# Experts' operands at one distance of 64 bytes, later casts of the row sums, and two short 32-bit products

## The chip, the cores and the metric

The kernel runs on one core of one Trainium2 chip. The metric is the device time of one execution in microseconds (us), the median over several runs. The engines are named as the profile names them: PE is TensorE's matmul, PEld its weight load, DVE is VectorE, ACT is ScalarE, POOL is GpSimd, SP is SyncE, which issues most of the DMAs.

## What is computed

The input is 8 sequences of 2496 tokens of 256 numbers. A Fourier layer mixes each sequence: real transform, a complex 256x256 product with a bias, a soft threshold, inverse transform. Its result goes through a mixture of 8 experts, in which every token takes one expert.

```python
X = np.fft.rfft(x, axis=1)
Yr = Xr @ w_r - Xi @ w_i + b_r
Yi = Xr @ w_i + Xi @ w_r + b_i
Y = soft_threshold(Yr, 0.01) + 1j * soft_threshold(Yi, 0.01)
x = np.fft.irfft(Y, n=2496, axis=1).reshape(19968, 256)

e_idx = argmax(x @ w_gate + modality_bias[modality_id])
for e in range(8):                       # w1: 8 x 256 x 1024, w2: 8 x 1024 x 256
    h = maximum(x[e_idx == e] @ w1[e], 0)
    out[e_idx == e] = gate_w * (h @ w2[e])
```

## The kernel before

The first 597 us are the Fourier layer and the routing: each sequence is transformed by matmuls, and its rows are scattered by expert into a table `xs` in HBM. The rest of the span is class `Experts`, and the change lies there.

**Units.** The experts' rows are worked on in 40 units, counted from 0: 38 of 512 rows and 2 of 256. Every operand is split into a rounded high part and a remainder (`xh`, `xl`; `hh`, `hl`; two slots in each weight tile), so a product of two matrices is three matmuls in a 32-bit format that TensorE takes in one pass, each with 128x128 stationary and 256 moving columns. Layer one (line 1024) holds the weights `w` stationary and streams `xh` or `xl`; layer two (line 1095) holds `hh` or `hl` stationary and streams `w`. From unit 8 on (`NPL` = 8) layer one is done with sums of rows and columns in 7 products in place of 8. A unit below 8 has 96 matmuls of layer one and 96 of layer two; units 8 to 37 have 84 and 96; the last two have 48 and 48. That makes 768 + 2520 + 96 = 3384 of layer one and 3648 + 96 = 3744 of layer two, 7128 in all.

**The order.** It is written out by hand in `run`. A unit has two groups (`grp` 0 and 1). In each, products of layer one of one half and of layer two of another take turns by the string that `order` gives ("1212..."; each "1" or "2" is 6 matmuls). After step n of a group the tables `FILL`, `FILL1`, `FILL2` say which side work is issued: "x" is one part of the next unit's split (an ACT cast to `xh`, line 958, and a POOL subtraction to `xl`, line 959), "t" the sums of rows on DVE, "o" an output, "p" DVE transposes for the unit after. Engines take their work in this order. Every sixth unit from unit 14 on also carries a small tile of at most 32 rows (`tiny`), whose few 32-bit matmuls stand between those blocks of 6.

**Where the operands lie.** Two sets of weight tiles take turns by the parity of the unit: set 1 lies behind the tiles of `xh`/`xl` and `hh`/`hl` on the left side of SBUF, set 0 at its right end. `PADS` shifts pools by a few floats. All tiles are multiples of 512 bytes long or are read at offsets that are, so an operand's start, taken modulo 512 bytes within its partition, is the same for all its slices. In the program as built these are:

| operand | role | before | after, odd unit | after, even unit |
|---|---|---|---|---|
| `xh`, `xl` | moving in layer one | 416 | 384 | 384 |
| `w0`, `w1` | stationary in layer one | 480 | 448 | 480 |
| `w2`, `w3` | moving in layer two | 480 | 384 | 416 |
| `hh`, `hl` | stationary in layer two | 416 | 448 | 448 |

While one matmul streams its moving operand, PEld loads the stationary operand of the next.

**Pads.** `setup_pads` fills a tile with a marker row; `pads` writes it behind each expert's rows, with the generator `late` as the caller, stepped once after some steps of a group (`LATE`).

Of the kernel before, what the change touches and what calls it, by code (L numbers as in the profile page):

```python
# [9 lines left out]
F32 = mybir.dt.float32  # L10
F32R = mybir.dt.float32r
# [12 lines left out]
D = 256  # L24
# [7 lines left out]
GC = D + E  # L32
# [8 lines left out]
TINY = 32  # L41
SLOTS = 5
MORE = 16
NPL = 8
EARLY = (6 * SEQ - 8 * (TP - 1)) // TP + 1 - E
PADS = (56, 16)
W1 = 2 * 2 * 4 * 128
W2 = 2 * 4 * 256
RAW = (2, 4, 6, 8, 10)
# [747 lines left out]
class Experts:  # L797
# [8 lines left out]

    def sets(self, ctx, i, **k):
        p = ctx.enter_context(self.tc.tile_pool(name=f"mw{i}", bufs=1, reuse_waits="tile", **k))
        return [p.tile([128, 2, 2, 7, 128] if n < 2 else [128, 2, 4, D], F32R, name=f"w{n}_{i}") for n in range(4)]

    def pools(self, ctx):
        nc, tc, rt = self.nc, self.tc, self.rt
        pool = lambda name, bufs, **k: ctx.enter_context(
            tc.tile_pool(name=name, bufs=bufs, reuse_waits="tile", **k))
        pad = lambda name, n: n and pool(name, 1).tile([128, n], F32, name=name + "t")
        self.x = pool("mx", 2)
        self.tr = pool("mtr", 1)
        self.cp = pool("mc", 1)
        self.ident = self.cp.tile([128, 128], F32, name="mident")
        nc.gpsimd.memset(self.ident, 0.0)  # L820
        nc.gpsimd.affine_select(out=self.ident, in_=self.ident, compare_op=ALU.not_equal, fill=1.0, base=0,
                                pattern=[[-1, 128]], channel_multiplier=1)
        pad("mq0", PADS[0])
        self.xp = pool("mxs", 1)
        self.s = pool("ms", 1)
        self.h = [pool("mh0", 1), pool("mh1", 1)]
        pad("mq1", PADS[1])
        self.wb.append(self.sets(ctx, 1))
        self.b = pool("mb", 2)
        room = rt.at.x1f[0]  # L830
        self.raw = (room[:, :2 * F].rearrange("p (c f) -> p c f", c=2),
                    room[:, 2 * F:2 * F + 8 * D].rearrange("p (c d) -> p c d", d=D))
        self.small, o = {}, 2 * F + 8 * D
        for nm, n in (("xt", GC), ("xc", 256), ("x", 256), ("hs", 256), ("h", 256), ("y", 256), ("ix", 1)):
            self.small[nm], o = room[:, o:o + n], o + n
        self.ps = pool("mps", 2, space=PSUM)
        self.hps = pool("mhps", 1, space=PSUM)
# [282 lines left out]
    def fill(self, n):  # L1120
# [3 lines left out]
        for _ in range(n):  # L1124
            self.nc.tensor.matmul(ps, tri[:, :128], tri[:, :512], start=True, stop=True)

    def put(self, ix, o):
        ins = self.nc.gpsimd.indirect_dma_start(  # L1128
            out=self.out, out_offset=bass.IndirectOffsetOnAxis(ap=ix, axis=0),
            in_=o, in_offset=None, bounds_check=NTOK - 1, oob_is_err=False)  # L1130
        self.tc.declare_no_dep(ins.ins, group="outs", reason="every token has one writer")
        self.tc.add_to_no_dep_group("outs", ins.ins)
# [74 lines left out]
    def sort_half(self, i):  # L1207
# [9 lines left out]
    FILL1 = {0: "x", 1: "o", 4: "x", 7: "x", 13: "x"}  # L1217
    FILL2 = {0: "x", 1: "o", 3: "t", 4: "x", 6: "x", 9: "x", 10: "x", 14: "x", 15: "x"}
    FILL = (
        {0: "x", 1: "o", 3: "t", 4: "x", 6: "xx", 8: "x", 11: "x", 13: "x"},  # L1220
        {1: "o", 3: "p", 5: "p"})
    LATE = (2, 3, 5, 7, 9, 10, 12)

# [9 lines left out]
    def run(self, late, *tail):  # L1233

        nc = self.nc
        U = NP + NS
        self.tags = {NPL - 1: [2, 4, 5, 6]}
        for i in range(NPL - 2, -1, -1):
            t = self.tags[i + 1]
            self.tags[i] = [t[3]] + [j for j in range(7) if j not in t]  # L1240
        pieces = self.weight_sums()
        for i in range(2):
            self.load_x(i)
        self.rt.setup_pads(self.cp.tile([128, GC], F32, name="pad2"))
        self.rt.grid2 = self.rt.load_grid(self.cp, "c_grid2", 5 * E + 3)
        for n in range(4):
            self.load_w(1, n)
            if n == 0:
                next(pieces)
        self.fold = self.cp.tile([128, TINY], F32, name="fold")  # L1250
        with self.tc.issue_after(tail[0].ins), self.tc.issue_after(tail[1].ins):
            for _ in chain(self.prep(0), self.sums(0), self.parts(0)):
                pass
        nc.vector.reduce_sum(self.fold, self.ident.rearrange("p (g t) -> p t g", t=TINY), AX.X)
        self.fill(5)
        for _ in self.layer1(0, 0):
            pass
        for _ in self.prep(1):
            pass
        every = (U - 8) // SLOTS  # L1260
        for i in range(U):
            if i + 2 < U:
                assert i + 2 < EARLY or self.rt.late
                if i == NPL - 2:
                    assert next(pieces, None) is None
                self.load_x(i + 2)
                self.load_w(i + 2, 0)
            k, at = divmod(U - 2 - i, every)
            k = U + SLOTS - 1 - k
            small = U <= k < U + SLOTS  # L1270
            if small and at == 2:
                self.load_x(k)
                self.stage = self.load_raw(k)
            if small and at == 1:
                self.sort_half(k)
            if small and at == 0:
                self.side = self.tiny(k)
            for grp in range(2):
                one = self.layer1(i + grp, 1 - grp) if i + grp < U else iter(())
                n1 = (8 if i + grp < NPL else 7 if i + grp < NP else 4) if i + grp < U else 0  # L1280
                n2 = 2 * self.subs(i)
                two = self.layer2(i, grp)
                fill = {"o": iter(()), "x": self.parts(i + 1) if grp == 0 and i + 1 < U else iter(()),
                        "t": self.sums(i + 1) if grp == 0 and i + 1 < U else iter(()),
                        "p": self.prep(i + 2) if grp == 1 and i + 2 < U else iter(())}
                if self.rest:
                    fill["o"], self.rest = self.last(*self.rest), None
                fills = self.FILL[grp] if grp or i >= NPL else self.FILL2 if i == NPL - 1 else self.FILL1
                for n, c in enumerate(self.order(n1, n2)):
                    next(one if c == "1" else two)  # L1290
                    for f in fills.get(n, ""):
                        next(fill[f], None)
                    if n in self.LATE:
                        next(late, None)
                    if i < NPL - 2:
                        next(pieces, None)
                    if c == "2":
                        next(self.stage, None)
                        if n % 3 == 0:
                            next(self.side, None)  # L1300
                for g in (one, two, fill["o"], fill["t"], fill["x"], fill["p"]):
                    for _ in g:
                        pass
                if i + 2 < U:
                    if grp == 0:
                        self.load_w(i + 2, 1)
                    self.load_w(i + 2, 2 + grp)
        for _ in self.side:
            pass
        self.finish(*self.rest)  # L1310

        k = U + SLOTS
        more = nc.values_load(self.rt.ti[k:k + 1, 3:4], min_val=0, max_val=1,
                              skip_runtime_bounds_check_because="a flag")
        with self.tc.If(more > 0):
            for i in range(k, k + MORE):
                self.load_x(i)
                for _ in self.load_raw(i):
                    pass
                self.sort_half(i)  # L1320
                self.half(i)
# [37 lines left out]
def build(tc, I, out, nb):  # L1359
    nc = tc.nc  # L1360
    with ExitStack() as outer:
# [218 lines left out]
        with ExitStack() as ctx:  # L1580
            ctx.enter_context(tc.manual_schedule(engines={ET.PE, ET.Activation, ET.DVE, ET.Pool}))
            ex.pools(ctx)

            def late():
                for state in chain(routing, rt.tiles_last(ex.cp)):
                    yield
                    if state == "pe":
                        for _ in range(3):
                            yield
                while rt.pending:  # L1590
                    rt.scatter(1)
                    yield
                    yield
                for _ in range(12):
                    yield
                rt.pads()
                for _ in range(8):
                    yield
                rt.fence()
                rt.late = True  # L1600


            ex.run(late(), *tail)
# [24 lines left out]
```

## Time and profile before

| | us |
|---|---|
| median of 3 runs | 1458.16 |
| lowest, highest | 1457.96, 1460.24 |
| the profiled execution | 1462.81 |
| its span, first to last instruction | 1460.9 |
| PE busy | 1427.8 |
| PEld busy | 1366.1 |
| DVE busy | 900.3 |
| ACT busy | 782.0 |
| POOL busy | 793.0 |

The profile is of one execution. Busy time of PE is the union of its matmuls, each of which is shown some 280 ns long though one starts about every 116 ns; what a matmul costs is therefore read from the distance between two starts. The timeline merges equal neighbours ("x2"), gives each row's start and length in us, and in square brackets the idle time ahead of it with what ended it.

### The profile page before, as it was taken

What the parts mean: (1) busy time and instruction counts of PE and PEld (TensorE: products, weight loads), DVE (VectorE), ACT (ScalarE), POOL (GpSimd) and SP (SyncE); (2) the same over time, 40 slices, a digit from 0 to 9 for tenths busy, and PEclk for the clock granted to TensorE, in tenths of its full rate; (3) what the DMA queues carried; (4) which work ended last, traced back from release to release, by engine and by line L of the source; (5) the groups of instructions that cost most, each with busy time, mean ns of one, the idle gap of its engine ahead of it and who ended that gap; (6) DMA issues with size and microseconds to landing.
All of it is one profiled execution on the core that took longest, in us unless ns stands there. A gap on an engine that the chain in (4) does not pass through costs nothing. (4 is left out here: it accounts for less than half of the span.)

```text
span 1460.9 us, 33883 instructions
## 1 busy us (share of the span) xinstructions
PE 1427.8 (98%) x12084; PEld 1366.1 (94%) x12084; DVE 900.3 (62%) x1721; ACT 782.0 (54%) x1675; POOL 793.0 (54%) x907
## 2 busy tenths in 40 slices
PE   8899999999999999999999999999999999999996
PEld 5889999998989999999999999999999999999995
DVE  4567575757575876667565665666566656665651
ACT  3465656565656454544445555555555555555542
POOL 2355767676767666366667543444344444444432
PEclk9999999999999999999999999999999999999998
DMA  8979686969696759687787288124122942682192
GB/s 265 264 236 297 212 284 214 298 215 299 200 297 182 224 180 290 198 248 249 240 277 245 70 291 268 38 59 115 32 60 58 338 126 59 203 261 59 44 355 80
DMA packets 245299, 289.82 MB, mean 198 GB/s; under 512 B 121232, under 2 KB 176267, under 8 KB 241925
## 3 DMA queue, kind: packets, MB, share of 16 engines
q1 hardware_dynamic: 225587, 244.64, 54.4%
q0 software_dynamic: 19408, 42.83, 9.3%
q8 instruction: 98, 1.61, 0.5%
q14 instruction: 76, 0.62, 0.1%
q10 hardware_dynamic: 130, 0.12, 0.0%
HBM read 322.80 MB, written 117.56 MB: 301 GB/s over the span
## 5 line engine op out<-in xcount | busy, mean ns | idle before, releaser
L1095 PE MATMUL y<-w,hh 128*128 128x256 f32 x2496 | 461.4, 279 | 0.0
L1095 PEld LDWEIGHTS y<-w,hh 128*128 128x128 f32 x2496 | 380.8, 189 | 3.7 <-issue 3.7
L1095 PE MATMUL y<-w,hl 128*128 128x256 f32 x1248 | 346.8, 278 | 1.1 <-DVE hl L1030 0.9
L1024 PE MATMUL X<-xh,w 128*128 128x256 f32 x1248 | 270.3, 281 | 0.0
L1128 POOL DMA_INDIRECT out<-o,ix x156 | 155.4, 996 | 182.4 <-ACT o L1112 145.7
L1095 PEld LDWEIGHTS y<-w,hl 128*128 128x128 f32 x1248 | 234.2, 188 | 1.7 <-DVE hl L1030 1.7
L1024 PEld LDWEIGHTS X<-xh,w 128*128 128x128 f32 x1248 | 212.6, 188 | 2.0 <-ACT hh L1029 1.6
L1024 PE MATMUL X<-xl,w 128*128 128x256 f32 x624 | 174.6, 280 | 0.6 <-POOL xl L959 0.6
L1030 DVE SCALAR_TENSOR_TENSOR hl<-Y,hh 128x512 fp32r<-128x512 f32 x140 | 96.8, 692 | 102.9 <-ACT hh L1029 102.8
L1029 ACT ACTIVATE hh<-Y 128x512 fp32r<-128x512 f32 x140 | 83.8, 599 | 119.0 <-DVE Y L1033 101.1
L959 POOL TENSOR_TENSOR xl<-tr,xh 128x256 fp32r<-128x256 f32 x94 | 70.4, 749 | 129.2 <-ACT xh L958 128.7
L1024 PE MATMUL Z<-xh,w 128*128 128x256 f32 x608 | 131.8, 281 | 0.7 <-DVE Y L1033 0.7
L382 PE MATMUL mx<-wmix,Xh 128*128 128x256 f32 x640 | 116.6, 305 | 7.5 <-DVE mx L372 7.2
L959 POOL TENSOR_TENSOR xl<-xt,xh 128x256 fp32r<-128x256 f32 x122 | 89.5, 746 | 58.5 <-ACT xh L958 57.2
L1024 PEld LDWEIGHTS X<-xl,w 128*128 128x128 f32 x624 | 117.1, 188 | 1.0 <-POOL xl L959 0.8
L1038 ACT COPY v<-X 128x512 f32<-128x512 f32 x180 | 105.6, 587 | 17.5 <-PE X L1024 10.3
L598 POOL DMA_INDIRECT xs<-x1b,si x88 | 90.0, 1023 | 41.5 <-DVE pl L430 19.6
L424 PE MATMUL pv<-pv,z 128*120 128x136 f32 x704 | 108.5, 279 | 1.0 <-ACT z L414 0.9
L598 POOL DMA_INDIRECT xs<-x,si x88 | 89.5, 1017 | 36.0 <-issue 16.7
L292 POOL TENSOR_TENSOR x1l<-x,x1h 117x512 fp32r<-117x512 f32 x59 | 75.6, 1284 | 60.8 <-ACT x1h L290 21.9
L382 PEld LDWEIGHTS mx<-wmix,Xh 128*128 128x128 f32 x640 | 92.4, 190 | 16.4 <-ACT x1h L290 3.6
L1024 PEld LDWEIGHTS Z<-xh,w 128*128 128x128 f32 x608 | 103.7, 188 | 0.9 <-DVE Y L1033 0.9
(261 smaller groups left out, 3435.8 us busy)
## 6 DMA issues: line engine op xcount, KB each, us to landing
w<-wsp SPq DMA_DIRECT2D x96, 1024.0 KB
w<-wss SPq DMA_DIRECT2D x64, 1024.0 KB
w<-wsp SPq DMA_DIRECT2D x64, 768.0 KB
a<-scr SPq DMA_DIRECT2D x160, 128.0 KB
x<-in_x SPq DMA_DIRECT2D x38, 512.0 KB
xt<-xs SPq DMA_DIRECT2D x152, 128.0 KB
scr<-ev SPq DMA_DIRECT2D x35, 480.0 KB
wsp<-wh SPq DMA_DIRECT2D x64, 256.0 KB
```

The lines of the kernel that those rows point to most:

```text
L292: (nc.gpsimd if pool else nc.vector).tensor_sub(xl, x, xh)
L382: nc.tensor.matmul(mx[:, i, :], t[:, c, 1 - i, :], self.w[:, i, c, lo, :], start=False, stop=n == 5, skip_group_check=True)
L424: nc.tensor.matmul(ps[:PK, c * 128:c * 128 + D // 2 + E], self.z[:, o:o + 3, :, :].rearrange("p n k r -> p (n k r)"), self.pv[:, c, :], st ...
L598: i = self.nc.gpsimd.indirect_dma_start(out=self.xs, out_offset=bass.IndirectOffsetOnAxis(ap=si[:, k:k + 1], axis=0), in_=rows, in_offset= ...
L959: (nc.gpsimd if i or j in (0, 1, 6) else nc.vector).tensor_sub(sq(xl), v, sq(xh))
L1024: nc.tensor.matmul(ps[:, u, :], w1[:, lo, u, blk, :], x, start=start and u == k == 0, stop=k == 2, skip_group_check=True)
L1029: nc.scalar.activation(hh[:, par::2, o], v, AF.Relu)
L1030: nc.vector.scalar_tensor_tensor(hl[:, par::2, o], v, 0.0, hh[:, par::2, o], ALU.max, ALU.subtract)
L1038: nc.scalar.copy(v, ps)
L1095: nc.tensor.matmul(ps, h[:, q, o], w2[:, lo, q, :], start=grp == s % 2 == q == k == 0, stop=grp == 1 and q == 3 and k == 2, skip_group_che ...
L1128: ins = self.nc.gpsimd.indirect_dma_start(out=self.out, out_offset=bass.IndirectOffsetOnAxis(ap=ix, axis=0), in_=o, in_offset=None, bounds ...
```

## The change

Five things are done. (1) In `sets`, the tiles `w2`, `w3` are laid out ahead of `w0`, `w1`, with a tile of 64 bytes between them; `pools` moves the pad of 64 bytes ahead of `hh`/`hl` and adds one of 448 bytes behind. With the 1056 bytes of the tile `pad2`, which goes, this gives the starts in the table above. (2) `FILL`, the table of units from 8 on, issues the casts after the second one step later or two. (3) `part` is new: one product in full 32-bit format, `fold` (128x32) stationary and `ident` (128x128) moving, into a PSUM tile that nobody reads. It stands after the first block of layer one in group 0 of units 1 and 9. (4) `setup_pads` of the experts' stage is called from `late`, one step ahead of `pads`, into a piece of an older tile. (5) The list of pads has a third entry.

```diff
-PADS = (56, 16)
+PADS = (56, 16, 112)
...
-        return [p.tile([128, 2, 2, 7, 128] if n < 2 else [128, 2, 4, D], F32R, name=f"w{n}_{i}") for n in range(4)]
+        w2 = [p.tile([128, 2, 4, D], F32R, name=f"w{n}_{i}") for n in (2, 3)]
+        p.tile([128, 16], F32, name=f"mq2_{i}")
+        return [p.tile([128, 2, 2, 7, 128], F32R, name=f"w{n}_{i}") for n in (0, 1)] + w2
...
         self.s = pool("ms", 1)
+        pad("mq1", PADS[1])
         self.h = [pool("mh0", 1), pool("mh1", 1)]
-        pad("mq1", PADS[1])
+        pad("mq3", PADS[2])
         self.wb.append(self.sets(ctx, 1))
...
+    def part(self):
+
+        ps = self.rt.ps.tile([128, 512], F32, tag="r", name="part")[:TINY, :128]
+        self.nc.tensor.matmul(ps, self.fold, self.ident, start=True, stop=True)
...
-        {0: "x", 1: "o", 3: "t", 4: "x", 6: "xx", 8: "x", 11: "x", 13: "x"},
+        {0: "x", 1: "o", 3: "t", 4: "x", 7: "x", 8: "x", 10: "x", 12: "x", 14: "x"},
...
-        self.rt.setup_pads(self.cp.tile([128, GC], F32, name="pad2"))
...
+                    if n == 1 and grp == 0 and i in (1, NPL + 1):
+                        self.part()
                     next(one if c == "1" else two)
...
-                for _ in range(12):
+                for _ in range(11):
                     yield
+                rt.setup_pads(ex.small["xt"])
+                yield
                 rt.pads()
```

PE at the start of group 0 of unit 1, before. `X_1` is a PSUM bank of layer one's second half, `y_0` the output bank of layer two; `w_1` are weights of set 1.

```order
L1024 MATMUL X_1_8734<-xh_1_8415,w_1_8245 128x256
L1024 MATMUL X_1_8734<-xl_1_8416,w_1_8245 128x256
L1024 MATMUL X_1_8734<-xh_1_8415,w_1_8245 128x256 x2
L1024 MATMUL X_1_8734<-xl_1_8416,w_1_8245 128x256
L1024 MATMUL X_1_8734<-xh_1_8415,w_1_8245 128x256
L1095 MATMUL y_0_8748<-w_1_8246,hh_1_8559 128x256 x2
L1095 MATMUL y_0_8748<-w_1_8246,hl_1_8560 128x256
```

The same place of PE now (lines 1024 and 1095 have become 1027 and 1098).

```order
L1027 MATMUL X_1_8737<-xh_1_8418,w_1_8253 128x256
L1027 MATMUL X_1_8737<-xl_1_8419,w_1_8253 128x256
L1027 MATMUL X_1_8737<-xh_1_8418,w_1_8253 128x256 x2
L1027 MATMUL X_1_8737<-xl_1_8419,w_1_8253 128x256
L1027 MATMUL X_1_8737<-xh_1_8418,w_1_8253 128x256
L1133 MATMUL part<-mident,fold 32x128
L1098 MATMUL y_0_8753<-w_1_8249,hh_1_8562 128x256 x2
L1098 MATMUL y_0_8753<-w_1_8249,hl_1_8563 128x256
```

One 32-bit product has come between the first block of layer one and the first of layer two; the same is so in unit 9, and nothing else of PE's order differs.

ACT in group 0 of unit 9, before: `xh_10` are casts for unit 10, `v_9` and `hh_9` are the copies and the relu that empty layer one's banks.

```order
L958 CAST xh_10_11499<-tr_11316 128x256
L958 CAST xh_10_11518<-xt_11097 128x256
L958 CAST xh_10_11522<-xt_11097 128x256
L1038 COPY v_9_1_11538<-X_1_11438 128x512
L1029 ACTIVATE hh_9_11436<-Y_1_11439 128x2x256
L958 CAST xh_10_11543<-xt_11097 128x256
L1029 ACTIVATE hh_9_11436<-X_1_11438 128x2x256
```

The same place of ACT now.

```order
L961 CAST xh_10_11506<-tr_11321 128x256
L961 CAST xh_10_11531<-xt_11102 128x256
L1041 COPY v_9_1_11541<-X_1_11443 128x512
L1032 ACTIVATE hh_9_11441<-Y_1_11444 128x2x256
L961 CAST xh_10_11546<-xt_11102 128x256
L961 CAST xh_10_11566<-xt_11102 128x256
L1032 ACTIVATE hh_9_11441<-X_1_11443 128x2x256
```

The copy of a bank and the relu behind it have moved ahead of one cast; this repeats in units 8 to 38.

## Rows read from the trace of the kernel before

**Rows 1.** The page's first part: busy us, share of the span, instructions.
```profile
PE 1427.8 (98%) x12084; PEld 1366.1 (94%) x12084; DVE 900.3 (62%) x1721; ACT 782.0 (54%) x1675; POOL 793.0 (54%) x907
```

**Rows 2.** Windows, PE: stretch, length, busy (x), PEclk, DMA share, GB/s.
```profile
932.00:1038.00 106.00, 106.00 (x913) 1.00 0.30 71
```

**Rows 3.** Timeline, PE, unit 0: start us, us, engine line operation.
```profile
599.15 0.28 PE L1024 MATMUL Y<-xh,w 128*128 128x256 f32 x1
...
601.87 0.28 PE L1024 MATMUL X<-xh,w 128*128 128x256 f32 x1
```

**Rows 4.** Timeline, PE, where blocks of the two layers take turns.
```profile
643.63 0.39 PE L1095 MATMUL y<-w,hh 128*128 128x256 f32 x2
...
644.32 0.28 PE L1024 MATMUL Z<-xh,w 128*128 128x256 f32 x1
...
645.03 0.40 PE L1095 MATMUL y<-w,hh 128*128 128x256 f32 x2
...
645.74 0.28 PE L1024 MATMUL Z<-xh,w 128*128 128x256 f32 x1
...
646.43 0.39 PE L1095 MATMUL y<-w,hh 128*128 128x256 f32 x2
```

**Rows 5.** Timeline, PE, in a double block of layer two, unit 17.
```profile
992.09 0.40 PE L1095 MATMUL y<-w,hh 128*128 128x256 f32 x2
...
993.15 0.28 PE L1024 MATMUL X<-xh,w 128*128 128x256 f32 x1
```

**Rows 6.** Timeline, PE, a small tile's 32-bit products and layer one behind.
```profile
923.60 1.07 PE L1196 MATMUL y<-x 128*32 128x256 f32 x16
...
924.95 0.39 PE L1024 MATMUL X<-xh,w 128*128 128x256 f32 x2
...
925.40 0.39 PE L1095 MATMUL y<-w,hh 128*128 128x256 f32 x2
```

**Rows 7.** Timeline, PE, its last 32-bit product and layer two behind.
```profile
928.76 0.28 PE L1095 MATMUL y<-w,hl 128*128 128x256 f32 x1
928.97 0.62 PE L1202 MATMUL ysum<-x,fold 128*32 128x256 f32 x2
...
929.86 0.28 PE L1095 MATMUL y<-w,hl 128*128 128x256 f32 x1
...
930.33 0.28 PE L1024 MATMUL X<-xh,w 128*128 128x256 f32 x1
```

**Rows 8.** Timeline, PE, the two waits and what follows the second.
```profile
727.73 0.38 PE L1095 MATMUL y<-w,hl 128*128 128x256 f32 x1 [0.94 <-DVE hl L1030]
...
906.84 0.39 PE L1024 MATMUL Z<-xh,w 128*128 128x256 f32 x1 [0.71 <-DVE Y L1033]
...
907.18 0.40 PE L1024 MATMUL Z<-xh,w 128*128 128x256 f32 x2
...
907.53 0.28 PE L1024 MATMUL Z<-xh,w 128*128 128x256 f32 x1
```

**Rows 9.** Timeline, DVE, ahead of the same two waits.
```profile
726.31 0.43 DVE L983 TENSOR_TENSOR bs<-br 128x256 f32<-128x256 f32 x1 [5.66 <-issue]
...
904.89 1.30 DVE L910 STREAM_TRANSPOSE tr<-xt 128x512 f32<-128x512 f32 x2 [3.58 <-DMA xt<-xs]
```

**Rows 10.** Timeline, PE, a short pause without a wait.
```profile
1003.59 0.30 PE L1024 MATMUL X<-xh,w 128*128 128x256 f32 x1
1003.73 0.28 PE L1024 MATMUL X<-xl,w 128*128 128x256 f32 x1
```

**Rows 11.** Timeline, ACT, the two casts and the copy behind them.
```profile
1002.20 0.77 ACT L958 CAST xh<-xt 128x256 fp32r<-128x256 f32 x2 [1.62 <-POOL xl L959]
1002.87 0.58 ACT L1038 COPY v<-X 128x512 f32<-128x512 f32 x1
```

**Rows 12.** Line 614, the pads' fill: duration ns least/median/most, first and last start.
```profile
L614 POOL MEMSET pad<- x2: 309/330/351, 539.6 to 582.7; 128x264 f32 x2
```

**Rows 13.** Page, part 5, POOL's subtraction: count | busy us, mean ns | idle before, releaser.
```profile
L959 POOL TENSOR_TENSOR xl<-tr,xh 128x256 fp32r<-128x256 f32 x94 | 70.4, 749 | 129.2 <-ACT xh L958 128.7
```

## The prediction, made before the changed kernel ran

> **What bounds the kernel now.** I read the page's busy times first, then windows over the experts' stage, then the timeline of PE alone, start by start. PE is busy 98% of the span, DVE, the next, 62% [rows 1], and in 932 to 1038 us PE is busy for all of 106.00 us at the full granted clock [rows 2]. So nothing on another engine can shorten this stage unless PE's own matmuls start closer together. How close they start is the question. The window counts 913 matmuls that touch it; one is shown 0.28 us long, so their starts fill 106.28 us: 116.4 ns from start to start.
>
> That is a mean of two paces. In unit 0, where layer one runs alone, 24 products go from 599.15 to 601.87 us: 2.72 us, 113.3 ns each [rows 3]. In a double block of layer two 9 products go from 992.09 to 993.15: 117.8 ns each [rows 5]. Shape, number format and clock are the same. Where blocks of six take turns, four in a row take 0.69, 0.71, 0.71 and 0.69 us: layer two fast, layer one slow, layer two slow, layer one fast [rows 4]. So the pace changes each time layer one follows layer two (644.32, 645.74), and is kept each time layer two follows layer one (645.03, 646.43). The reader is to see that nothing waits there: it is an offset that the stream of matmuls carries on until something shifts it.
>
> **Why the operands' places would matter.** By the table of starts, inside a block of layer one PE streams from 416 while PEld loads from 480, and inside layer two the reverse. At a boundary both read from the same start: 416 and 416 going from one to two, 480 and 480 going from two to one. Only there, and only at the second kind, does the pace change. This is a reading of rows, no proof. After the change every pair, inside and across, streams from the 64 bytes that begin at 384 and loads from those that begin at 448 (even units lie 32 bytes further in some of them). If the reading holds, blocks no longer change the pace, and whatever pace an outside event leaves stays.
>
> **Which pace is left.** Behind the small tile's 16 short 32-bit products layer one starts fast: 4 products from 924.95 to 925.40, 112.5 ns [rows 6]. Behind its last 32-bit product, with the same `fold` as the new `part`, layer two starts slow: 4 from 929.86 to 930.33, 117.5 ns [rows 7]. Layer one is the case with the stream in the lower place; after the change layer two is so too, so I expect it fast behind both, and behind `part`.
>
> **The sum, by stretch.** A fast product gains 116.4 - 113.3 = 3.1 ns, a slow one loses 117.8 - 116.4 = 1.4 ns.
> Until `part` in unit 1 (about 626 us) I can't tell the pace: 0.
> From there to PE's wait at 727.73 [rows 8]: some 101 us, 865 products fast: -2.7 us.
> From that wait to `part` in unit 9 (about 803 us): behind the other wait layer one runs 3 products in 0.35 us, 117 ns [rows 8], so I take slow: 650 x 1.4 = +0.9.
> From 803 to the wait at 906.84: 880 products fast: -2.7.
> From there through the small tile at 929 [rows 7]: mixed, 0.
> Units 14 to 37 behind it: 24 x 180 = 4320 products. Four further small tiles cover some 155 products each; on these 620 I count half, -1.0; on the other 3700 -11.5. The last two units: 0.
> Together -17.0 us. The most there could be is 7128 x 3.1 = 22.1.
>
> **What is added.** *The two products.* From 928.76 to 929.86 stand one product ahead of `ysum`, `ysum` itself and two behind: 1.10 us where three products take 0.35, so 0.75 us for 256 moving columns [rows 7]. `part` has 128. Between half and all of it I take 0.5 each, nearer to the half, as the columns are: +1.0 (0.75 to 1.5). It is on the path, since PE has no gap.
>
> *Pauses.* At 1003.59 a matmul starts 0.14 us after the one ahead without a wait being shown [rows 10]; there is one more of this kind in the later units. Before, a changed offset was undone or repeated a block later; after, a slow one would stay until the next small tile, at most five units, half of that on average: 450 x 4.5 ns = 2.0 us. I count half of one such case, +1.0 (0 to 4).
>
> *The two waits.* PE waits 0.94 and 0.71 us for DVE [rows 8], and DVE in its turn had waited for data: 5.66 us ahead of an addition that reads a loaded tile, 3.58 us for the DMA of an `xt` [rows 9]. If these data come no earlier, what PE gained ahead of them, 2.7 us each time, is given back there. The loads are mostly issued behind PE's own steps and so move with it; I take +1.0 for both (0 to 5.4).
>
> *Casts.* ACT's copy of layer one's bank starts at 1002.87, behind two casts that began at 1002.20 [rows 11]; with one cast moved behind it, it starts some 0.37 us earlier. PE was not waiting for it [rows 2], so the gain is 0. The last cast moves from step 13 to 14, and DVE's transposes, which overwrite its source, come after step 3 of the next group: four blocks of 0.70 us, 2.8 us, less a cast of 0.4 [rows 11] and POOL's 0.75 [rows 13], leave 1.6 us. That room is the cover. Were it gone, the transposes would hold up the `hl` queued behind them on DVE, for which layer two waits: up to the 0.7 us of the shift in a unit, 31 times, 22 us. I see no row that points to it.
>
> *Pads.* The fill of 0.33 us [rows 12] moves on POOL's queue from the start of the stage to the step ahead of the pads. Behind it on POOL stand outputs, and SP's pad writes wait for it; units that read them come later. POOL is busy 54% [rows 1]: 0 to 0.4, I take 0.
>
> **Sum.** -17.0 + 1.0 + 1.0 + 1.0 = -14.0 us. The profiled execution took 1462.81, so 1448.8 for it; the median of the runs is 4.65 lower, 0.3%, and 1458.16 - 14.0 gives 1444.
>
> **Rivals.** *Slow pace kept.* The same mechanism, with the other outcome: behind `part` and the small tiles the common pace is the slow one, as layer two's was [rows 7], and now nothing flips it back. All products at 117.8 ns cost 7128 x 1.4 = 10.0 us, and `part` 1.0: 1469. It decides where the share of fast products falls under 1.4 / 4.5 = 31%; before, it is about that much, since the mean is 116.4 between 113.3 and 117.8. For it speaks that I know the outcome behind a 32-bit product only for the old places; against it, layer one's fast start [rows 6] in the very arrangement that is now common to all. Chance 0.16, of which 0.03 ends below 1461.
>
> *Places don't matter.* The flips come from something else, the alternation stays as it is, and `part` costs its 1.0: 1459. Against it speaks that only one of the two boundaries flips [rows 4], and that a run of one layer never does [rows 3]. Chance 0.10.
> [...]
>
> *Gain given back.* Fast pace, but both waits take all that was won ahead of them, 5.4 in place of 1.0, and two pauses leave the slow pace: 1444 + 4.4 + 3.0 = 1451. It lies within the forecast's case.
>
> **How the numbers follow.** The forecast's case, mostly fast, has 0.74. Its best end is 22.1 less 0.75, 1437; I leave 0.04 below 1438. Its worst, with small tiles leaving the slow pace now and then, is 1455. Range 1438 to 1461: left out are 0.04 below and 0.13 above. About 0.2% (3 us) is what a measurement of this kernel can tell from no change. Faster 0.74, same 0.10, slower 0.16.
>
> **What would show it.** In the changed profile, blocks of six all 0.68 us long in units 1 to 6, 9 to 12 and from 15 on, with no step where layer one follows layer two, would show the places' part right; one even length of 0.71 would show the slow rival, and 0.69, 0.71, 0.71, 0.69 as before the third. The first block behind `part` shows whether it sets the pace, and the first behind PE's waits near 727 and 906 us whether a wait unsets it. What would make the forecast wrong at its root is a slow pace behind the small tiles, since two thirds of the gain lie between them.

## The result, and the profile after

| | before | after |
|---|---|---|
| median, us | 1459.93 | 1470.71 |
| lowest, highest, us | 1457.96, 1461.46 | 1469.2, 1473.06 |
| span of the profiled execution, us | 1460.9 | 1468.2 |
| PE busy, us | 1427.8 | 1437.5 |

The changed kernel is slower: 1.0077 times the time before, 95% interval 1.0061 to 1.0092, or 10.8 us, where 14 us less was forecast. The page's first part of after, to lay beside [rows 1]:

```profile
PE 1437.5 (98%) x12088; PEld 1375.7 (94%) x12088; DVE 896.5 (61%) x1721; ACT 783.6 (53%) x1675; POOL 792.0 (54%) x907
```

PE has four instructions more (each `part` is two) and 9.7 us more of work; no other engine has taken over. The window that [rows 2] shows of before, in after (stretch, length, PE busy and count, granted clock, DMA share, GB/s):

```profile
932.00:1038.00 106.00, 106.00 (x901) 1.00 0.30 71
```

PE again has no gap and the full clock, but 901 matmuls touch the window where 913 did: 106.28 / 901 = 118.0 ns from start to start, against 116.4. That is not the fast pace (113.3), and it is a little above the slow one of [rows 5] (117.8). So the mean is where the time went: 7128 products at 1.4 to 1.6 ns more are 10 to 11.4 us.

The timeline of PE in after shows that the pace is not one. First the place of the first `part`, in unit 1 (start us, us, engine, line, operation):

```profile
622.38 0.28 PE L1027 MATMUL X<-xh,w 128*128 128x256 f32 x1
622.59 0.41 PE L1133 MATMUL part<-mident,fold 128*32 128x128 f32 x2
622.93 0.51 PE L1098 MATMUL y<-w,hh 128*128 128x256 f32 x2
623.27 0.28 PE L1098 MATMUL y<-w,hl 128*128 128x256 f32 x1
...
623.73 0.28 PE L1027 MATMUL X<-xh,w 128*128 128x256 f32 x1
...
633.25 0.28 PE L1027 MATMUL X<-xh,w 128*128 128x256 f32 x1
...
633.98 0.40 PE L1098 MATMUL y<-w,hh 128*128 128x256 f32 x2
...
634.67 0.28 PE L1027 MATMUL X<-xh,w 128*128 128x256 f32 x1
...
635.39 0.28 PE L1098 MATMUL y<-w,hh 128*128 128x256 f32 x1
```

From 623.73 to 633.25 stand 84 products in 9.52 us, 113.3 ns each, through 13 boundaries: just what the forecast expected everywhere. This is group 0 of unit 1, where every operand is of the odd set. At 633.25 group 1 begins, and layer one now works on unit 2, with the weights of the even set. At once it is slow (0.73 us for six, 122 ns; then 0.72, 120 ns), while layer two, still on unit 1, takes 0.69 (115 ns). Nothing waits here, and no other row comes between: the weights' set is what changed, and with it the distance of layer one's operands, from 64 bytes to 96.

Later in the program, units 16 and 17 (same columns):

```profile
955.59 0.40 PE L1098 MATMUL y<-w,hh 128*128 128x256 f32 x2
...
965.57 0.28 PE L1027 MATMUL X<-xh,w 128*128 128x256 f32 x1
...
976.90 0.40 PE L1098 MATMUL y<-w,hh 128*128 128x256 f32 x2
...
986.80 0.28 PE L1027 MATMUL X<-xh,w 128*128 128x256 f32 x1
```

Group 0 of unit 16, all of the even set, has 84 products between the first two rows: 9.98 us, 118.8 ns. Group 0 of unit 17, all of the odd set, has 84 between the last two: 9.90 us, 117.9 ns. The odd unit could run fast, as unit 1 did, but it takes over a slow pace and nothing in it turns that. The second `part`, in unit 9, stands in the same kind of place as the first and does not turn it either:

```profile
802.39 0.28 PE L1027 MATMUL X<-xh,w 128*128 128x256 f32 x1
802.60 0.41 PE L1133 MATMUL part<-mident,fold 128*32 128x128 f32 x2
802.94 0.51 PE L1098 MATMUL y<-w,hh 128*128 128x256 f32 x2
803.29 0.28 PE L1098 MATMUL y<-w,hl 128*128 128x256 f32 x1
...
803.76 0.28 PE L1027 MATMUL Y<-xh,w 128*128 128x256 f32 x1
...
804.47 0.40 PE L1098 MATMUL y<-w,hh 128*128 128x256 f32 x2
```

The block of layer one behind it takes 0.71 us. The two waits of [rows 8] have gone or shrunk with the slower PE. The list of PE's waits in the experts' stage of after has one entry left (us in total, times, longest), and that one stands near the end of the span:

```profile
PE X L1027 <- POOL xl L962: 0.6, 1, 0.6
```

### The profile page after: what moved, and what is told of

Read it like the earlier page. It is cut to its first block, busy times and chain, and to the rows that moved or that the text cites. A ratio compares the mean times of both kernels' runs of the same rounds, so it can differ in the third digit from the quotient of the medians.

```text
span 1468.2 us, 33893 instructions
## 1 busy us (share of the span) xinstructions
PE 1437.5 (98%) x12088; PEld 1375.7 (94%) x12088; DVE 896.5 (61%) x1721; ACT 783.6 (53%) x1675; POOL 792.0 (54%) x907
## 5 line engine op out<-in xcount | busy, mean ns | idle before, releaser
L1098 PE MATMUL y<-w,hh 128*128 128x256 f32 x2496 | 466.9, 281 | 0.0
L1098 PE MATMUL y<-w,hl 128*128 128x256 f32 x1248 | 350.7, 281 | 0.2
L1027 PE MATMUL X<-xh,w 128*128 128x256 f32 x1248 | 273.3, 282 | 0.0
L1027 PEld LDWEIGHTS X<-xl,w 128*128 128x128 f32 x624 | 117.5, 188 | 1.1 <-POOL xl L962 0.8
```

The source lines that it names most:

```text
L1027: nc.tensor.matmul(ps[:, u, :], w1[:, lo, u, blk, :], x, start=start and u == k == 0, stop=k == 2, skip_group_check=True)
L1098: nc.tensor.matmul(ps, h[:, q, o], w2[:, lo, q, :], start=grp == s % 2 == q == k == 0, stop=grp == 1 and q == 3 and k == 2, skip_group_che ...
```

## The experiments

All are compared with the kernel before on the same chip, by the ratio of times; the chips differ (the kernel before took 1486 us on the first, 1460.2 and 1458.6 on the others), so absolute times are compared only within a group.

### Are the places the loss, and is it the 32 bytes?

The rivals were the even units' 32 bytes, the pairs' new order as such, and the casts or `part`. Forecasts in us of this group were made for a kernel before of about 1458 us and are read here as ratios. Two kernels remove the 32 bytes in different ways. `even_moved` shifts the even set down by 32 bytes, so that all starts are 384 and 448:

```diff
-        return [p.tile([128, 2, 2, 7, 128], F32R, name=f"w{n}_{i}") for n in (0, 1)] + w2
+        w1 = [p.tile([128, 2, 2, 7, 128], F32R, name=f"w{n}_{i}") for n in (0, 1)]
+        if i == 0:
+            p.tile([128, 8], F32, name="mq4")
+        return w1 + w2
```

> The changed kernel, with set 0 (even units) 32 bytes lower, so that in every unit the moving operands start at 384 and the stationary ones at 448 (modulo 512 bytes). Theory A (the 32 bytes by which only the even units' weights are shifted break the fast pace): behind the short product of unit 1 the blocks of even and odd units keep 113.3 ns a product; most of the stage fast, 1436 to 1450 us. Theory B (the fast pace is lost whenever another set of weights comes in, or at random, whatever the 32 bytes): fast in group 0 of unit 1 alone, as in the changed kernel, 1466 to 1474 us.

Measured: 0.9932 (0.9907 to 0.9957), 1477.44 against 1486.01 us.

`left_moved` shifts everything on the left side up instead, so that all starts are 416 and 480:

```diff
-PADS = (56, 16, 112)
+PADS = (64, 16, 112)
```

> The changed kernel, with everything on the left side 32 bytes higher instead: moving operands at 416, stationary ones at 480 in every unit, so one distance of 64 bytes, and all starts 32 bytes off a multiple of 64 as before the change. Theory A in its first form (only that the starts are alike in all units matters): as the kernel with set 0 moved, 1436 to 1450 us. Theory A2 (starts at a multiple of 64 matter too): above that kernel by more than 5 us. Theory B: 1466 to 1474 us.

Measured: 0.992 (0.9895 to 0.9946), 1473.44 us. Both turn a loss of 0.8% into a gain of 0.7 or 0.8%. Whether the pair of starts is 384 and 448 or 416 and 480 made no difference that could be told. In both kernels all units agree and all distances are 64 bytes; which of the two counts is asked further down.

The other two parts, apart. `places_alone` is the changed kernel with the old casts and without `part`:

```diff
-        {0: "x", 1: "o", 3: "t", 4: "x", 7: "x", 8: "x", 10: "x", 12: "x", 14: "x"},
+        {0: "x", 1: "o", 3: "t", 4: "x", 6: "xx", 8: "x", 11: "x", 13: "x"},
...
-                    if n == 1 and grp == 0 and i in (1, NPL + 1):
-                        self.part()
```

> The changed kernel with the casts at their old steps and without the two short products: of the change the operands' places and the later fill of the pads alone. Theory A: the places are the loss, and the short products gave at most some 10 us of fast pace: 1469 to 1473 us. Theory C (the loss comes from the later casts or from the short products): 1456 to 1462 us, as before.

Measured: 1.0071 (1.0047 to 1.0095): all of the loss. The later fill of the pads is in it, and in `even_moved` and `left_moved` as well; it was not priced alone.

`casts_alone` is the kernel before with the new `FILL`:

```diff
-        {0: "x", 1: "o", 3: "t", 4: "x", 6: "xx", 8: "x", 11: "x", 13: "x"},
+        {0: "x", 1: "o", 3: "t", 4: "x", 7: "x", 8: "x", 10: "x", 12: "x", 14: "x"},
```

> The kernel before, with the later casts as the only edit. Theory A: PE did not wait for those casts, 1458 to 1461 us, no difference. Theory C (the later casts cost): 1464 to 1472 us.

Measured: 0.9994 (0.9974 to 1.0014), no difference.

### Is it enough that all units agree?

`distance_128` makes all units alike, as `even_moved` does, but with 128 bytes in place of 64 between the two operands (`x`, `w2`, `w3` at 320, `h`, `w0`, `w1` at 448):

```diff
-PADS = (56, 16, 112)
+PADS = (40, 32, 96)
...
-        p.tile([128, 16], F32, name=f"mq2_{i}")
+        p.tile([128, 32], F32, name=f"mq2_{i}")
...
+        if i == 0:
+            p.tile([128, 8], F32, name="mq4")
```

> The kernel with set 0 moved, with 128 bytes in place of 64 between what is streamed and what is loaded, the same in all units (320 and 448). Theory A1 (all that counts is that starts are alike in all units and both layers): fast as with 64, 0.6 to 0.9% below the kernel before. Theory A2 (the streamed and the loaded line must differ by an odd number of 64 bytes): slow, blocks of 117.5 ns or more, 0.5 to 1.0% above the kernel before.

Measured: 1.0109 (1.0081 to 1.0137), slower than the change itself. A window of the same length in its trace, begun 8 us later, since a small tile's 32-bit product stands at 936.31 there:

```profile
940.00:1046.00 106.00, 106.00 (x895) 1.00 0.30 70
```

106.28 / 895 = 118.7 ns, as in group 0 of the even units of the change (118.8), but now as the mean over units of both parities. So it is not that units disagree: of the distances tried, the fast pace, 113.3 ns, was measured over whole groups at 64 bytes alone. Beside it on that chip the changed kernel itself, once more:

> The changed kernel unedited, for a comparison on the same chip as the next three. Theory A (the 32 bytes of the even units' weights break the fast pace): 0.6 to 0.9% above the kernel before, that is +9 to +13 us, with most blocks at 117 to 120 ns a product.

Measured: 1.007 (1.0046 to 1.0093), as the first time. The two intervals overlap, but the executions don't: 1475.93 to 1479.95 us with 128 bytes, 1466.09 to 1473.14 here.

### What are `part` and the casts worth when PE is fast?

`left_no_part` is `left_moved` without `part`:

```diff
-PADS = (56, 16, 112)
+PADS = (64, 16, 112)
...
-                    if n == 1 and grp == 0 and i in (1, NPL + 1):
-                        self.part()
```

> The kernel with the left side moved (one distance of 64 bytes in all units), without the two short products. Theory A: the pace is fast ahead of both short products in its trace, so they do no work there: within 2 us of the kernel with them, 0.7 to 0.9% below the kernel before. Theory P (the short products set the fast pace): units 1 to 8 slow, 7 to 8 us more than with them.

Measured: 0.9895 (0.9866 to 0.9924), 1444.35 us, where the kernel before took 1460.18 on that chip. The 7 to 8 us that Theory P adds didn't come; the gain is even larger than Theory A's 0.7 to 0.9%. It was run again beside `left_moved` on a third chip:

> The kernel with the left side's operands moved up by 32 bytes (even and odd units then agree in all differences) and without the two products of `part`, on one chip with the same kernel that has them, so that `part` is priced where PE is fast. Theory P0 (`part` costs what it takes on PE, some 0.4 us each, and the rest of the difference seen on two chips was the chips'): ratio 0.990 to 0.992 here, and the kernel with `part` at most 0.001 above. Theory P1 (`part` does more: behind it the engines around come late and PE waits, or the pace turns slow for a while): 0.9895 here as before, and the kernel with `part` 0.002 or more above it.

> The other half of the pair: the same places with `part` in units 1 and 9. P0: at most 1.5 us slower than without it (ratio at most 0.001 higher). P1: 3 us or more slower.

Measured: 0.9899 (0.9883 to 0.9916) without `part` and 0.9921 (0.9904 to 0.9938) with it, 1443.87 and 1447.13 us. The intervals overlap; the medians are 3.3 us apart, more than the two products' own time, which the trace with `part` shows to be short:

```profile
624.79 0.39 PE L1027 MATMUL X<-xh,w 128*128 128x256 f32 x2
...
625.13 0.28 PE L1027 MATMUL X<-xh,w 128*128 128x256 f32 x1
625.34 0.41 PE L1133 MATMUL part<-mident,fold 128*32 128x128 f32 x2
625.67 0.51 PE L1098 MATMUL y<-w,hh 128*128 128x256 f32 x2
626.01 0.28 PE L1098 MATMUL y<-w,hl 128*128 128x256 f32 x1
```

From 625.13 to 626.01 are 0.88 us where three products take 0.34: 0.54 each, 1.1 for both. The list of PE's waits has more of it. With `part`, then without (us in total, times, longest):

```profile
PE Z L1027 <- DVE Y L1036: 2.0, 1, 2.0
PE y L1098 <- DVE hl L1033: 1.2, 2, 1.0
```

```profile
PE Z L1027 <- DVE Y L1036: 1.2, 1, 1.2
PE y L1098 <- DVE hl L1033: 0.5, 2, 0.4
```

These are 1.5 us longer with `part` (3.2 against 1.7). Own time and waits make 2.6 of the 3.3 us; but in another execution of the kernel without `part` the same two entries were 1.7 and 2.0 us, so that the waits differ from one execution to the next as much as between these two. That `part` lengthens them is not shown. In this trace it has nothing to do, since PE is fast ahead of it too (three products from 624.79 to 625.13).

The longer of the waits is that of [rows 8] at 907, now earlier and longer. PE, and DVE ahead of it, in the kernel without `part`:

```profile
899.04 0.38 PE L1027 MATMUL Z<-xh,w 128*128 128x256 f32 x1 [1.21 <-DVE Y L1036]
```

```profile
897.09 1.30 DVE L913 STREAM_TRANSPOSE tr<-xt 128x512 f32<-128x512 f32 x2 [3.91 <-DMA xt<-xs]
898.32 0.67 DVE L1036 TENSOR_TENSOR Y<-Z,v 128x512 f32<-128x512 f32 x1
```

DVE stood 3.91 us for the rows of `xt` from HBM, and the sum that empties layer one's bank was queued behind the transposes of those rows.

Whether `part` is needed where the even set is moved, and what it does to the kernel before:

> The even units' weights moved down by 32 bytes (all starts at 384 and 448) without `part`. With `part` this gave 0.9932, and its trace had a slow stretch from about 662 us to a wait near 730. If `part` isn't what makes the pace fast once all places agree, it stays at 0.993 or a little under; if it is needed here, since a bf16 product of the routing leaves the slow pace at the stage's start, the slow pace lasts from there to the first wait or small tile, and the ratio is 0.995 or more.

```diff
+        if i == 0:
+            p.tile([128, 8], F32, name="mq4")
...
-                    if n == 1 and grp == 0 and i in (1, NPL + 1):
-                        self.part()
```

Measured: 0.9896 (0.988 to 0.9913), median 1444.56 us, but its four executions took 1441.1, 1444.19, 1444.92 and 1450.97, and the profile is of the longest. PE at the start of its stage, then two windows:

```profile
619.16 0.28 PE L1030 MATMUL Z<-xh,w 128*128 128x256 f32 x1
...
619.84 0.24 PE L565 MATMUL rk<-oh,tri 117*117 117x184 bf16 x1
...
620.82 0.28 PE L1030 MATMUL Z<-xh,w 128*128 128x256 f32 x1
...
621.53 0.40 PE L1101 MATMUL y<-w,hh 128*128 128x256 f32 x2
```

```profile
735.00:895.00 160.00, 160.00 (x1361) 1.00 0.73 236
...
925.00:1030.00 105.00, 105.00 (x923) 1.00 0.30 72
```

The six products ahead of the routing's bf16 rows take 0.68 us, the six of layer one behind them 0.71. In the first window 160.28 / 1361 = 117.8 ns, slow; the second, behind most of the first small tile, is fast (923 there and 928 in `left_no_part_2`; one more of the tile's 32-bit products, at 929, falls into it). So the slow start that the expectation feared is real in this execution and fits its extra 6 to 10 us; the other three have no trace. The expectation's end of the slow stretch of `even_moved`, near 730, is misread: that trace is slow from 662, behind one bf16 product, to a pause of 0.1 us at 755 (512 matmuls touch the 60 us from 665: 60.28 / 512 = 117.7 ns). At these places `part` may be an insurance; it isn't needed in the median.

> The kernel before with `part` alone in units 1 and 9. By the reading that at the old places the pace turns at each boundary from layer two to layer one, whatever it was, nothing lasts: the cost is the two products', some 0.4 us each, ratio 1.0003 to 1.001. If `part` does more by itself, such as a lasting slow pace, it is 1.003 or more.

```diff
+                    if n == 1 and grp == 0 and i in (1, NPL + 1):
+                        self.part()
```

Measured: 1.001 (0.9998 to 1.0022), 1.9 us by the medians, too little to tell from the products' 1.1 and from no difference.

`left_old_casts` is `left_moved` (with `part`) and the old `FILL`:

```diff
-PADS = (56, 16, 112)
+PADS = (64, 16, 112)
...
-        {0: "x", 1: "o", 3: "t", 4: "x", 7: "x", 8: "x", 10: "x", 12: "x", 14: "x"},
+        {0: "x", 1: "o", 3: "t", 4: "x", 6: "xx", 8: "x", 11: "x", 13: "x"},
```

> The kernel with the left side moved, with the casts at their old steps. Theory A: PE at its fast pace still doesn't wait for the casts, or shows two or three pauses of 25 ns, each able to set the slow pace until the next small tile: 0 to +4 us against the kernel with the later casts. Theory C (with a faster PE the old casts hold up layer one's banks): waits of PE for ACT in units 8 to 37 and over +4 us.

Measured: 0.9976 (0.9953 to 0.9999), 1456.88 us, so 0.0055 above `left_moved` with the later casts (8 us; the ratios are from different chips). The timelines of ACT and of PE in unit 16 show why:

```profile
949.74 0.71 ACT L961 CAST xh<-xt 128x256 fp32r<-128x256 f32 x2 [1.67 <-POOL xl L962]
950.36 0.58 ACT L1041 COPY v<-X 128x512 f32<-128x512 f32 x1
```

```profile
950.88 0.28 PE L1098 MATMUL y<-w,hl 128*128 128x256 f32 x1
950.99 0.38 PE L1027 MATMUL X<-xh,w 128*128 128x256 f32 x1
951.21 0.28 PE L1027 MATMUL X<-xl,w 128*128 128x256 f32 x1
...
951.80 0.40 PE L1098 MATMUL y<-w,hh 128*128 128x256 f32 x2
...
952.51 0.28 PE L1027 MATMUL Z<-xh,w 128*128 128x256 f32 x1
```

ACT's copy stands behind two casts and ends at 950.94. PE's next product into an `X` bank is shown 0.38 us long in place of 0.28, and the one behind it comes 0.22 us later in place of 0.11. That the copy is the cause shows by repetition: away from the small tiles and the waits this trace has 13 such pauses between 822 and 1383 us, each 0.05 or 0.06 us behind the end of such a copy, and the traces of `left_with_part_2`, `left_no_part` and `left_no_part_2`, with the later casts, have none. What follows costs more than this tenth: the next block takes 0.71 us, and the slow pace stays until the small tile's 16 short products at 1035.71. The window between, of this kernel and of `left_no_part_2`, which has the later casts:

```profile
955.00:1030.00 75.00, 75.00 (x639) 1.00 0.31 75
```

```profile
955.00:1030.00 75.00, 75.00 (x664) 1.00 0.31 77
```

25 products fewer in 75 us, 2.8 us lost behind one pause of 0.1. Two more stretches of this kind follow, from 1060 to 1166 (792 matmuls touch the 93 us from 1062: 117.8 ns) and from 1211 to 1296; behind the other ten pauses the pace stayed fast.

## Why the prediction was wrong, step by step

**What bounds the kernel, and the two paces: right.** PE was and is the bound, and 113.3 and 117.8 ns are the two regular paces. Which of them held went with the places: with nothing but places different, `distance_128` and `left_with_part_2` stand at 1.0109 and 0.9921, some 27 us apart. That decides against the rival "places don't matter".

**Where it failed.** It is the parenthesis "even units lie 32 bytes further in some of them". The prediction's own table showed it: in an even unit layer one streams from 384 and loads from 480, 96 bytes apart, and layer two streams from 416 and loads from 448, 32 apart. The prediction put both into the pieces of 64 bytes that begin at 384 and 448 and counted them as equal. They are not: group 0 of an even unit ran at 118.8 ns, and, as even units come every second time, each odd unit began with the slow pace that they left. The gain of -17.0 us was booked on nearly all units, and the fast pace held through a whole group only once, in group 0 of unit 1; in its place came a mean of 118.0 ns, a loss of 10 to 11.4 us. The step "places agree, so nothing flips the pace" should have been priced for an exact 64 and, separately, for the pairs 96 and 32, of which no row of before showed anything; the bound from the nearest rows would have been the slow pace.

**The slow rival: right in time, not in cause.** It gave 1469 from all products at 117.8 ns, and 1470.7 came; that the two lie so close is luck. Its mechanism was that `part` and the small tiles leave the slow pace, which nothing flips back. `part` in fact left the fast one, as forecast, in unit 1, and the slow one in unit 9. The small tiles did leave the slow one in after, but in `left_no_part_2` PE, too, comes slow out of a small tile's last 32-bit product, and a block later it is fast. Its timeline, for [rows 7]:

```profile
1047.75 0.62 PE L1210 MATMUL ysum<-x,fold 128*32 128x256 f32 x2
1048.30 0.50 PE L1098 MATMUL y<-w,hh 128*128 128x256 f32 x2
1048.64 0.28 PE L1098 MATMUL y<-w,hl 128*128 128x256 f32 x1
...
1049.11 0.28 PE L1027 MATMUL X<-xh,w 128*128 128x256 f32 x1
...
1049.79 0.39 PE L1098 MATMUL y<-w,hh 128*128 128x256 f32 x2
```

Four products of layer two from 1048.64 to 1049.11 at 117.5 ns, as in [rows 7], and then six of layer one in 0.68. So the forecast "fast behind both" was off by one block, and the step from layer two to layer one still turned a slow pace there. A slow pace that a pause leaves in layer one was not turned (the 75 us of `left_old_casts`).

**The sum, where its condition holds: nearly right.** With even and odd units alike and `part` in, the kernel stands at 0.9921, 11.5 us under the kernel before, where the sum had -14.0. `part`: 1.1 us on PE, forecast 1.0. The two waits: 3.2 us together where before had 1.65, so +1.5 in these two executions, forecast +1.0 with 5.4 at most. The rest, -14.1, is the pace by subtraction, where -17.0 and +1.0 for pauses were booked. One reading ahead of the waits was not shown: the 5.66 us of [rows 9] end with `issue`, which names no wait for data.

**Casts: right for the change, wrong as a rule.** "PE was not waiting for it, so the gain is 0" holds at the pace before in the time (0.9994), though not at two places: the pause in [rows 10] (the product at 1003.59 is followed by the next after 0.14 us, in place of 0.11) and the copy behind two casts in [rows 11] (it ends at 1003.45) are one event, and the prediction took them for two. Both pauses of this kind in before, at 1003.59 and 1370.88, start 0.14 us behind such a copy's end; `before_part` still has both, `casts_alone` neither. At the fast pace there are 13 (`left_old_casts`), by the author's reading because the copy's bank is needed sooner. It did foresee what a pause may cost, a slow pace up to the next small tile; it didn't see that the later casts are what removes it. The cost of their shorter cover, feared at up to 22 us, didn't appear: no run showed it.

**The test that it named itself.** "0.69, 0.71, 0.71, 0.69 as before" didn't come, nor one even length: the blocks are 0.69 and 0.72, or 0.70 to 0.72 irregularly, by the parity of the unit and its group. That outcome was on no list.

## What to carry to other kernels

When an argument needs operands in a certain relation, write down the relation for every pair, every buffer set and every boundary, and price each pair that differs as a case of its own; "nearly the same place" was the whole loss here, and eight floats of padding turned it into the gain (from 1.0077 to 0.9932 or 0.992). When the bounding engine gets faster, look again at the engines that feed it with little to spare: a cast order that was worth nothing before was worth some 8 us then. And a small pause without a listed wait is worth tracing to the engine that empties the bank.

## What the runs showed of the hardware

All at a granted clock of 1.00 in the windows shown, with one shape (128x128 stationary, 256 moving columns, 32-bit, one record in the trace for each product):

- The distance between starts of two such products was 113.3 ns where moving and stationary operand start 64 bytes apart (modulo 512) and the pace was fast, 117.8 to 117.9 at the same distance when the pace was slow, 118.8 with 96 and 32 in turn, 118.7 with 128. In one group with 96 in layer one and 64 in layer two, six took 0.72 and 0.69 us.
- At 64 bytes both paces were seen to last over hundreds of products: the slow one in `even_no_part` (160.28 us / 1361 = 117.8 ns), the fast one in `left_no_part_2` (75.28 / 664 = 113.4). The other pace stood behind a pause of 0.1 us in 3 of 13 cases in `left_old_casts` (0.71 us for the next six) and behind a bf16 product at 619.84 in `even_no_part` (0.68 us for six ahead, 0.71 behind). Behind a 32-bit product it was not the same each time: in one execution of the changed kernel the blocks took 0.70 us ahead of `part` and 0.68 behind it in unit 1, and 0.71 on both sides in unit 9.
- Moving both operands by 32 bytes (384 and 448, or 416 and 480) made no difference that could be told: 0.9896 and 0.9899 without `part`.

Why 64 bytes differ from 32, 96 and 128, and why the second `part` didn't turn the pace, the traces don't show; 32 or 96 bytes in all units, and distances of 192 bytes and more, were not tried.
